# Second half of the first queries: from casting loads on GpSimd's queue to fp32 loads on the sync engine's queue with a cast on VectorE

## The chip, the cores and the metric

The kernel runs on one core of one Trainium2 chip. The metric is the device time of one execution in microseconds. A profile of one execution stands beside the timed runs. Instructions are named by the engine that does them: TensorE (PE, its weight loads PEld), VectorE (DVE), ScalarE (ACT), GpSimd (POOL) and the sync engine (SP), which here only issues DMAs. A DMA issued by GpSimd goes to the queue that the profile calls q0 and may cast on its way; one issued by the sync engine goes to q1.

## The reference

```python
batch, n_heads, seq, head_dim = (4, 8, 768, 64);  n_blocks = 8
P = sort_net
for _ in range(5):                       # rows, then columns, made to sum to one
    P = exp(P - max(P, -1)); P /= sum(P, -1) + 1e-9; P /= sum(P, -2) + 1e-9
k_sorted = einsum('bhij,bhjcd->bhicd', P, k_blocks)      # blocks of 96 tokens
v_sorted = einsum('bhij,bhjcd->bhicd', P, v_blocks)
scores = q_blocks @ k_sorted_blocks.T / sqrt(64)
x = softmax(scores) @ v_sorted_blocks    # within each block
x = x.transpose(0, 2, 1, 3).reshape(3072, 512)
h = x @ w_in                             # 512 x 2048
out = (s * relu(h)**2 + b) @ w_out       # 2048 x 512, float32
```

All inputs are float32.

## The kernel before

The matrices are brought to bf16 and everything large runs on TensorE. The tokens of one batch element are done in two halves of 384 tokens (4 blocks of 96), so that there are eight halves t = 0 to 7. For each half there is an attention part and then two matrix products: `ffn1(t)` (x times w_in, relu, square, into the tile gt) and `ffn2(t)` (gt times w_out, then the store). The order of the instructions on each engine is the order in which the program text calls them: the schedule is written out by hand. Attention pieces of a later half are dropped between the matrix products through dictionaries of `slots`: a slot number says after which step of `ffn1` or `ffn2` a piece is called.

Batch element 0 has nothing before it to hide behind. Its start is: the five normalisations of `sort_net` on 32 partitions (VectorE and ScalarE in turn), the block matrix `PD[0]` on 128 partitions (L270), sorted keys (`k_piece`, tile tp into KS), sorted values (`v_piece`), transposed queries (`q_piece` for blocks 0 to 3, `q_blocks` for blocks 4 to 7 in two calls of two blocks), scores (`s_piece`, `s_banks`), exponentials, and the product with the values (`p_piece`). Then x is transposed (`t_piece`).

Loads of batch 0: the sync engine's queue takes `sort_net` (L79) and v as fp32 (L83). GpSimd's queue takes k (L93) and the first four query blocks (L111), each query block one DMA of 96 partitions by 8 heads by 64 numbers into QTOK, cast to bf16. Then `load_w` issues the weights, also on GpSimd and cast to bf16. `part(a, f)` is one eighth of w_in: rows a and a+1 (of four groups of 128) and a quarter f of the columns. GpSimd does its instructions in order, and `load_w` uses this: the copy L150 reads the block matrix PD[0], so that nothing after it is issued before PD[0] is there, and the copy L154 reads the last column of KS[0], so that nothing after it is issued before the sorted keys are complete. Between these stands the first w_in piece; after the second gate come two more pieces, the four loads of query blocks 4 to 7 (L111), five pieces, and w_out in four DMAs (L165). Loads for batch 1 follow on the same engine (L592 on). Eight semaphores are used in turn for GpSimd's DMAs, so that a DMA waits until the one eight places earlier has landed.

`ffn1(0)` starts with `ahead=3`: for the first three of its eight steps the products with row groups 0 and 1 are done first, then those with groups 2 and 3. Its slot -1 has `t_piece(0, 0, 2)` (transposes of x, evacuated by ScalarE and VectorE), slot ("pre", 1) has `q_blocks(0, 4)`, evacuated by VectorE, and slot 1 has `q_blocks(0, 6)`, evacuated by ScalarE. So on TensorE the 16 transposes of query blocks 4 to 7 (L333) come after the second step and before the third step's row groups 2 and 3. The evacuation and square of each step are

```python
nc.scalar.activation(out=rt, in_=h, func=AF.Relu)                                       # L511
nc.vector.tensor_tensor(out=gt[:, 2 * i:2 * i + 2, :], in0=rt, in1=rt, op=ALU.mult)     # L512
```

and then the slot's pieces are called.

Of the kernel before, what the change touches and what calls it, by code (L numbers as in the profile page):

```python
# [9 lines left out]
FP = mybir.dt.float32  # L10
# [12 lines left out]
def kernel(  # L23
# [12 lines left out]
    nc = tc.nc  # L36

    B, H, S, D = q.shape
    NB = sort_net.shape[-1]
    BLK = S // NB  # L40
# [5 lines left out]
    HB = NB // 2  # L46
    TG = HB * BLK
    C2 = BLK // 2
# [13 lines left out]
    const = ctx.enter_context(tc.tile_pool(name="const", bufs=1))  # L62
# [19 lines left out]
    for c in range(0, C2, CV):  # L82
        nc.sync.dma_start(out=v0f[:, c:c + CV, :].rearrange("p c d -> p (c d)"),  # L83
                          in_=raw[2][0][:, c * D:(c + CV) * D])
# [18 lines left out]
    QTOK = {}  # L103

    def load_q(b, ns=range(NB)):

        if b not in QTOK:
            QTOK[b] = rawp.tile([BLK, NB, H, D], BF, tag="rawq", name="qtok")
        qv = q[b].rearrange("h (n t) d -> t n h d", n=NB)
        for n in ns:  # L110
            nc.gpsimd.dma_start(out=QTOK[b][:, n], in_=qv[:, n])  # L111
# [5 lines left out]
    KS = [const.tile([128, NG, 2, GAP], BF, name=f"ks{i}") for i in range(2)]  # L117
# [17 lines left out]
    load_q(0, range(HB))  # L135
    ones = const.tile([128, 32], BF)
    sel = const.tile([128, 128], BF)
    wi = const.tile([128, NHP, d_ff], BF)
    wo = const.tile([128, NF, d_model], BF)

    def load_w():
        wiv = moe_w_in.rearrange("(a p) f -> p a f", p=128)
        fq = d_ff // 4

        def part(a, f):
            nc.gpsimd.dma_start(out=wi[:, a:a + 2, f * fq:(f + 1) * fq],  # L146
                                in_=wiv[:, a:a + 2, f * fq:(f + 1) * fq])


        nc.gpsimd.tensor_copy(out=ones[:, 0:1], in_=PD[0][:, 0, 0, 0:1])  # L150
        nc.gpsimd.memset(KS[1][:, :, :, C2:GAP], 0.0)
        nc.gpsimd.memset(sel, 0.0)
        part(0, 0)
        nc.gpsimd.tensor_copy(out=ones[:, 0:1], in_=KS[0][:, 0, 0, C2 - 1:C2])  # L154
        part(0, 1)
        part(2, 0)
        load_q(0, range(HB, NB))
        part(2, 1)
        for f in (2, 3):
            for a in (0, 2):  # L160
                part(a, f)
        wov = moe_w_out.rearrange("(f p) n -> p f n", p=128)
        for c in range(4):
            fs = slice(c * (NF // 4), (c + 1) * (NF // 4))
            nc.gpsimd.dma_start(out=wo[:, fs, :], in_=wov[:, fs, :])  # L165
# [14 lines left out]
    def permute(eng, src, cs=slice(0, C2), ds=slice(0, D)):  # L180
# [3 lines left out]
        else:  # L184
# [12 lines left out]
            out=jsel, in_=ident.rearrange("p (h j z) -> p j h z", h=H, j=NB), axis=AX.XY, op=ALU.add),  # L197
        lambda: nc.vector.tensor_reduce(
            out=bm.rearrange("p (e z a) -> p e z a", e=2, z=2),
            in_=idv.rearrange("p a e j z -> p e z a j"), axis=AX.X, op=ALU.add),  # L200
    ] + [
        lambda z=z: nc.vector.tensor_copy(
            out=emat[:, 1:B, z * 64:(z + 1) * 64].rearrange("p b (h j) -> p b h j", h=H),
            in_=ident[0:BH, H:B * H].rearrange("p (b h) -> p b h", b=B - 1).unsqueeze(3).broadcast_to(
                [BH, B - 1, H, NB]))
# [121 lines left out]
    def q_blocks(b, n0, eng):  # L327

        ps = psb.tile([128, 1024], BF, tag="b", name="tqb")
        for n in range(2):  # L330
            for hp in range(NHP):
                c0 = (n * NHP + hp) * BLK
                nc.tensor.transpose(  # L333
                    out=ps[:, c0:c0 + BLK],
                    in_=QTOK[b][:, n0 + n, 2 * hp:2 * hp + 2, :].rearrange("p h d -> p (h d)"),
                    identity=ident[0:BLK, 0:BLK])
        evac(eng, q_tile(b)[:, n0:n0 + 2].rearrange("p n a t -> p (n a t)"),
             ps[:, 0:2 * NHP * BLK])
# [119 lines left out]
    def t_piece(b, half, hp2, eng):  # L458

        x = X[b, half]  # L460
        if hp2 == 0:
            XT[b * 2 + half] = xtp.tile([128, HB, NHP, BLK], BF, tag="xt", name="xt")
        n = HB // len(eng)
        for i, g in enumerate(eng):
            tr = psb.tile([128, 1024], BF, tag="b", name="tr")
            for hp in (hp2, hp2 + 1):
                for m in range(n):
                    c0 = (m * 2 + hp % 2) * BLK
                    nc.tensor.transpose(out=tr[:, c0:c0 + BLK],
                                        in_=x[:, i * n + m, hp * 128:(hp + 1) * 128],  # L470
                                        identity=ident[0:BLK, 0:BLK])
            evac(g, XT[b * 2 + half][:, i * n:(i + 1) * n, hp2:hp2 + 2, :],
                 tr[:, 0:n * 2 * BLK].rearrange("p (n a c) -> p n a c", n=n, a=2))
# [10 lines left out]
    def ffn1(t, slots, ahead=0):  # L484

        gt = gtp.tile([128, NF, TG], BF, tag="gt", name="gt")
        GT[t] = gt
        xt = XT[t]
        H1 = {}

        def part(i, hpl):
            if i not in H1:
                H1[i] = psa.tile([128, 2, 512], FP, tag="a", name="hps")
            for f in range(2):
                for hp in hpl:
                    fc = (2 * i + f) * 128
                    nc.tensor.matmul(out=H1[i][:, f, 0:TG], lhsT=wi[:, hp, fc:fc + 128],  # L497
                                     rhs=xt[:, :, hp, :],
                                     start=(hp == 0), stop=(hp == NHP - 1))

        for i in range(ahead):
            for p in slots.get(i - ahead, ()):
                p()
            part(i, (0, 1))
        for i in range(NF // 2):
            part(i, (2, 3) if i < ahead else range(NHP))
            for p in slots.get(("pre", i), ()):
                p()
            rt = rtp.tile([128, 2, TG], BF, tag="rt", name="rt")
            h = H1.pop(i)[:, :, 0:TG]  # L510
            nc.scalar.activation(out=rt, in_=h, func=AF.Relu)  # L511
            nc.vector.tensor_tensor(out=gt[:, 2 * i:2 * i + 2, :], in0=rt, in1=rt, op=ALU.mult)  # L512
            for p in slots.get(i, ()):
                p()
# [41 lines left out]
    k_piece(0, CK, "D")  # L556
    k_piece(0, 2 * CK, "A")
    load_w()
    v_piece(0, 0, "A")
    q_piece(0, 0, "D")  # L560
# [72 lines left out]
    def SB(b, h, i): return lambda: s_banks(b, h, i)  # L633
    def P(b, h, i): return lambda: p_piece(b, h, i)
    def TP(b, h, i, eng): return lambda: t_piece(b, h, i, eng)
    def TD(b, h): return lambda: t_dma(b, h)
    def PDB(b): return lambda: build_pd(b)
    def QB(b, n0, eng): return lambda: q_blocks(b, n0, eng)


    ffn1(0, {-1: [TP(0, 0, 2, "AD")], ("pre", 1): [QB(0, HB, "D")], 1: [QB(0, HB + 2, "A")],
             2: [SB(0, 1, 0)], 3: [SB(0, 1, 1), P(0, 1, 0)], 4: [SB(0, 1, 2), P(0, 1, 1)],
             5: [SB(0, 1, 3), P(0, 1, 2)], 6: [TP(0, 1, 0, "D"), P(0, 1, 3)]}, ahead=3)
    ffn1(1, {-2: [TP(0, 1, 2, "D")], 1: [masks_z, lambda: take_p(1, B - 1, PB, jselz), PDB(1)], 4: [PDB(2), sum_w],
# [20 lines left out]
    for b in range(B):  # L665
        n = b + 1
# [55 lines left out]
```

## Time and profile before

| what | us |
|---|---|
| median of 3 runs (lowest, highest) | 223.7 (223.66, 227.12) |
| the profiled execution | 224.31 |
| its span, from first to last instruction of the program | 222.5 |
| TensorE busy | 214.8 |
| VectorE busy | 116.6 |
| ScalarE busy | 100.8 |
| GpSimd busy (DMA issues among it) | 55.2 |

The times of the views count from the start of the span; the profiled execution has 1.8 us around it. In a timeline the columns are start, length, engine, line, operation, what is written and read, shape and count, and in brackets the idle time of the engine before it and what ended it. In the DMA views a queue's numbers are packets, megabytes and the share of 16 DMA engines; bytes and packet sizes are those written. Times to landing run from the issue to the last byte's semaphore.

### The profile page before, as it was taken

What the parts mean: (1) busy time and instruction counts of PE and PEld (TensorE: products, weight loads), DVE (VectorE), ACT (ScalarE), POOL (GpSimd) and SP (SyncE); (2) the same over time, 40 slices, a digit from 0 to 9 for tenths busy, and PEclk for the clock granted to TensorE, in tenths of its full rate; (3) what the DMA queues carried; (4) which work ended last, traced back from release to release, by engine and by line L of the source; (5) the groups of instructions that cost most, each with busy time, mean ns of one, the idle gap of its engine ahead of it and who ended that gap; (6) DMA issues with size and microseconds to landing.
All of it is one profiled execution on the core that took longest, in us unless ns stands there. A gap on an engine that the chain in (4) does not pass through costs nothing.

```text
span 222.5 us, 5383 instructions
## 1 busy us (share of the span) xinstructions
PE 214.8 (97%) x2307; PEld 127.1 (57%) x2307; DVE 116.6 (52%) x237; ACT 100.8 (45%) x132; POOL 55.2 (25%) x99
## 2 busy tenths in 40 slices
PE   7898889999999999999999999999999999999993
PEld 8886556655555545655555545665455566654453
DVE  6857547599938556443426746444244734442122
ACT  4688476565442326663354136664325055650000
POOL 8349787359030009100040019000000000000000
PEclk9999999999999999999999999999999999999999
DMA  5999999999979769999669869969423240001212
GB/s 178 258 95 131 163 203 207 219 193 132 177 137 219 147 165 122 156 112 211 160 134 202 209 155 141 151 133 207 114 78 72 102 111 4 0 0 47 94 50 94
DMA packets 66744, 30.51 MB, mean 137 GB/s; under 512 B 57440, under 2 KB 61920, under 8 KB 66528
## 3 DMA queue, kind: packets, MB, share of 16 engines
q0 software_dynamic: 30832, 12.85, 47.3%
q1 hardware_dynamic: 35888, 17.31, 34.4%
q8 instruction: 18, 0.29, 0.5%
q14 instruction: 6, 0.05, 0.1%
HBM read 29.63 MB, written 8.65 MB: 172 GB/s over the span
## 4 chain that ended last, share of the span: by engine, by line
PE 86%; DMA 4%; DVE 4%; POOL 2%; ACT 2%; issue 1%; POOLq 0%
PE ops L522 36%; PE hps L497 36%; DMA wi<-in_moe_w_in_dram 3%; PE pv L441 3%; PE tp L295 2%; PE sc L406 2%; PE ops L536 2%; POOL qtok L111 1%; PE tv L379 1%; ACT ks L284 1%; DMA sne<-in_sort_net_dram 1%; POOL wi L146 1%; PE vob L360 1%; ACT sne L213 1%; DVE rstat L223 1%
## 5 line engine op out<-in xcount | busy, mean ns | idle before, releaser
L497 PE MATMUL hps<-xt,wi 128*128 128x384 bf16 x512 | 86.4, 326 | 1.3 <-DMA wi<-in_moe_w_in_dram 0.9
L522 PE MATMUL ops<-wo,gt 128*128 128x512 bf16 x368 | 84.9, 379 | 0.0
L511 ACT ACTIVATE rt<-hps 128x768 bf16<-128x768 f32 x64 | 51.6, 811 | 52.9 <-PE hps L497 52.0
L497 PEld LDWEIGHTS <-wi 128*128 128x128 bf16 x512 | 48.9, 98 | 35.4 <-issue 2.5
L512 DVE TENSOR_TENSOR gt<-rt 128x768 bf16<-128x768 bf16 x64 | 38.4, 602 | 44.0 <-ACT rt L511 41.9
L522 PEld LDWEIGHTS <-gt 128*128 128x128 bf16 x368 | 34.0, 98 | 37.6
L544 DVE SCALAR_TENSOR_TENSOR ot<-ops,s_bc,bias 128x512 f32<-128x512 f32 (+2 forms) x26 | 18.4, 706 | 33.5 <-PE ops L522 31.5
L411 ACT ACTIVATE at<-sc 96x768 bf16<-96x768 f32 (+1 forms) x28 | 21.2, 806 | 28.4 <-PE sc L406 28.4
L111 POOL DMA_DIRECT2D qtok<-in_q_dram x32 | 24.8, 786 | 7.5 <-DMA wo<-in_moe_w_out_dram 3.7
L449 DVE TENSOR_TENSOR x<-pv,rec 96x512 bf16<-96x512 f32 x32 | 22.0, 687 | 1.1
L441 PEld LDWEIGHTS <-at 112*128 112x128 bf16 (+3 forms) x256 | 10.9, 101 | 4.3 <-ACT vs L284 0.9
L441 PE MATMUL pv<-vs,at 112*128 112x66 bf16 (+3 forms) x256 | 11.7, 195 | 0.8 <-DVE vs L286 0.8
L176 PE MATMUL z<-zeros 128*128 128x142 bf16 (+1 forms) x114 | 11.0, 268 | 1.2 <-DVE zeros L115 1.2
L448 DVE RECIPROCAL rec<-pv 96x8 f32<-96x8 f32 x32 | 6.3, 198 | 11.2 <-PE pv L441 11.2
L284 ACT CAST ks<-tp 128x1024 bf16<-128x1024 f32 x8 | 8.1, 1012 | 7.4 <-PE tp L295 7.4
L176 PEld LDWEIGHTS <-zeros 128*128 128x128 bf16 x114 | 9.5, 116 | 1.4 <-DVE zeros L114 1.0
L661 POOL COPY gate<-gt 128x1 bf16<-128x1 bf16 x2 | 0.4, 191 | 36.8 <-DVE gt L512 36.8
L406 PEld LDWEIGHTS <-ks 64*128 64x128 bf16 x224 | 5.2, 94 | 5.1 <-issue 2.1
L286 DVE CAST ks<-tp 128x1024 bf16<-128x1024 f32 x4 | 4.9, 1222 | 5.7 <-PE tp L295 5.7
L406 PE MATMUL sc<-qt,ks 64*128 64x96 bf16 x224 | 7.5, 204 | 0.2 <-DVE x L449 0.2
L295 PEld LDWEIGHTS <-rawk 128*64 128x64 bf16 x384 | 6.4, 113 | 1.7 <-issue 1.3
L295 PE MATMUL tp<-pd,rawk 128*64 128x64 bf16 x384 | 6.8, 196 | 0.0
(105 smaller groups left out, 117.9 us busy)
## 6 DMA issues: line engine op xcount, KB each, us to landing
out_dram<-ot SPq DMA_DIRECT2D x23, 256.0 KB, 2.1
qtok<-in_q_dram POOLq DMA_DIRECT2D x32, 96.0 KB, 7.2
rawk<-in_k_dram POOLq DMA_DIRECT2D x6, 384.0 KB, 10.3
rawv<-in_v_dram POOLq DMA_DIRECT2D x6, 384.0 KB, 6.6
dv<-VO SPq DMA_DIRECT2D x12, 192.0 KB, 6.4
vs<-dv SPq DMA_DIRECT2D x2, 1152.0 KB, 7.2
wi<-in_moe_w_in_dram POOLq DMA_DIRECT2D x8, 256.0 KB, 8.1
wo<-in_moe_w_out_dram POOLq DMA_DIRECT2D x4, 512.0 KB, 13.8
```

The lines of the kernel that those rows point to most:

```text
L111: nc.gpsimd.dma_start(out=QTOK[b][:, n], in_=qv[:, n])
L176: nc.tensor.matmul(out=Z[0][:, 0:w], lhsT=zeros[:, 0:128], rhs=zeros[:, 0:w], start=True, stop=True)
L295: nc.tensor.matmul(out=ps[e * 64:(e + 1) * 64, c].rearrange("p z g -> p (z g)"), lhsT=src[:, c0 + c, :], rhs=mov[:, e].rearrange("p z g -> ...
L406: nc.tensor.matmul(out=sc[:, e, n * BLK:(n + 1) * BLK], lhsT=KS[b % 2][pr, g0 + n].rearrange("p z c -> p (z c)"), rhs=QT[b][pr, half * HB ...
L411: nc.scalar.activation(out=at, in_=sc[0:rows(b), :, 0:TG], func=AF.Exp, scale=scale)
L441: nc.tensor.matmul(out=pv[0:m, e, n * VW:(n + 1) * VW], lhsT=atf[:, c0:c0 + m], rhs=VS[b > 1][:, e * NG + g0 + n, 0:VW], start=True, stop= ...
L449: nc.vector.tensor_tensor(out=x[:, :, hp * 128:(hp + 1) * 128].rearrange("p n (e d) -> p e n d", e=2), in0=pvv[:, :, :, 0:D], in1=rec.unsq ...
L497: nc.tensor.matmul(out=H1[i][:, f, 0:TG], lhsT=wi[:, hp, fc:fc + 128], rhs=xt[:, :, hp, :], start=(hp == 0), stop=(hp == NHP - 1))
L511: nc.scalar.activation(out=rt, in_=h, func=AF.Relu)
L512: nc.vector.tensor_tensor(out=gt[:, 2 * i:2 * i + 2, :], in0=rt, in1=rt, op=ALU.mult)
L522: nc.tensor.matmul(out=ops, lhsT=gt[:, f, m * 128:(m + 1) * 128], rhs=wo[:, f, :], start=(f == 0), stop=(f == NF - 1))
L544: nc.vector.scalar_tensor_tensor(out=ot[:, ns], in0=ops, scalar=s_bc, in1=BIAS[0][:, ns], op0=ALU.mult, op1=ALU.add)
```

## The change

The copy L154, the second gate on GpSimd, is taken out. The loads of query blocks 4 to 7 leave GpSimd: the sync engine issues four DMAs into a new fp32 tile q0f. A memset of four numbers per partition of q0f stands on GpSimd behind the second w_in piece; since the loads overwrite what it wrote, the first of them waits for it. Two VectorE casts, each of two blocks, bring q0f into QTOK; they stand in slot -1 of `ffn1(0)`, after the transposes of x. Everything else is as it was.

```diff
+    q0f = const.tile([BLK, HB, H, D], FP)
     wi = const.tile([128, NHP, d_ff], BF)
     wo = const.tile([128, NF, d_model], BF)
...
         nc.gpsimd.memset(sel, 0.0)
         part(0, 0)
-        nc.gpsimd.tensor_copy(out=ones[:, 0:1], in_=KS[0][:, 0, 0, C2 - 1:C2])
         part(0, 1)
+        nc.gpsimd.memset(q0f[:, :, 0, 0:1], 0.0)
+        qv = q[0].rearrange("h (n t) d -> t n h d", n=NB)
+        for n in range(HB):
+            nc.sync.dma_start(out=q0f[:, n], in_=qv[:, HB + n])
         part(2, 0)
-        load_q(0, range(HB, NB))
         part(2, 1)
...
+    def cast_q(n):
+
+        nc.vector.tensor_copy(out=QTOK[0][:, HB + n:HB + n + 2], in_=q0f[:, n:n + 2])
+
-    ffn1(0, {-1: [TP(0, 0, 2, "AD")], ("pre", 1): [QB(0, HB, "D")], 1: [QB(0, HB + 2, "A")],
+    ffn1(0, {-1: [TP(0, 0, 2, "AD"), lambda: cast_q(0), lambda: cast_q(2)], ("pre", 1): [QB(0, HB, "D")], 1: [QB(0, HB + 2, "A")],
```

In the changed kernel the lines after these stand three to eight places further down: the transposes L333 are L336, the relu L511 is L514, the square L512 is L515.

## The prediction

> **What bounds the kernel now.** I read the page first: TensorE is busy for 214.8 of 222.5 us, so only time in which TensorE stands still can be won. Next, the chain that ended last in order of time, to see where it leaves TensorE after the start:
>
> ```profile
> 15.88 0.28 issue
> 16.15 1.42 POOL wi L146 x2
> 17.57 3.06 POOL qtok L111 x4
> 20.62 7.77 DMA wi<-in_moe_w_in_dram
> 28.40 0.05 issue
> 28.44 0.82 PE hps L497 x4
> ```
>
> Columns are start, length, what. The changed issues are on the chain: four query loads take GpSimd 3.06 us ahead of the fourth w_in piece, which lands at 28.40 us and releases TensorE. The table of waits prices that:
>
> ```profile
> PE hps L497 <- DMA wi<-in_moe_w_in_dram: 0.9, 1, 0.9
> ```
>
> One wait of 0.9 us is all that an earlier w_in can remove directly. Next, the timelines of TensorE and VectorE at that place:
>
> ```profile
> 24.67 2.17 PE L497 MATMUL hps<-xt,wi 128*128 128x384 bf16 x12
> 26.67 0.85 PE L333 MATMUL tqb<-ident,qtok 96*128 96x96 bf16 x16
> 28.44 0.82 PE L497 MATMUL hps<-xt,wi 128*128 128x384 bf16 x4 [0.93 <-DMA wi<-in_moe_w_in_dram]
> ```
>
> ```profile
> 24.87 0.36 DVE L286 COPY xt<-tr 128x384 bf16<-128x384 bf16 x1 [0.52 <-PE tr L469]
> 27.06 0.56 DVE L512 TENSOR_TENSOR gt<-rt 128x768 bf16<-128x768 bf16 x1 [1.84 <-ACT rt L511]
> ```
>
> TensorE transposes the second queries at 26.67; from 28.44 on it is nearly always busy. So the deadline of the second queries is 26.67 us, in bf16. VectorE has a free slot of 1.84 us just before.
>
> Last, the DMA queues, since a load changes queue. Three stretches: 5 to 9 us (v on the sync engine's queue against k on GpSimd's), 87.5 to 89.5 us (dv stores against query loads), 28.4 to 40 us (weights alone):
>
> ```profile
> q0 software_dynamic: 239, 0.46, 60.5%
> q1 hardware_dynamic: 245, 0.69, 47.9%
> ...
> q0 software_dynamic: 897, 0.11, 85.8%
> q1 hardware_dynamic: 885, 0.17, 76.2%
> ...
> q0 software_dynamic: 2391, 2.36, 123.3%
> ```
>
> q0 is GpSimd's, q1 the sync engine's; the first number counts packets. When both have work, they move the same number of packets, whatever the packets' size. The price of sharing shows in dv, whose transfers need 2.6 us with the engines to themselves and up to 9.7 us beside the query loads:
>
> ```profile
> DMA to landing us min/median/max: 2.6/6.9/9.7
> ```
>
> **What the Trainium skill says.** "DMA: Bandwidth & Descriptors", section "Issuing engines are not separate DMA queues": transfers of all engines run on the same 16 DMA engines and interleave. The trace agrees (dv above). Its section "Queues, rings and completion order": each DMA engine goes round-robin between queues at packet granularity, typically 9 to 17 descriptors a turn. The trace agrees on the turns; its equal counts, with records as large as 3 KB against 2 KB and as small as 192 B against 128 B, look like one record a turn. "VectorE: DVE Perf Modes", section "The perf-mode tier table": an fp32 copy within SBUF runs at 2 elements a cycle; the 512-element cast L619 took 426 ns, which fits. "TensorE: Matmul & The Clock Gate", section "Part 1: The HAM clock gate": after an idle window of some 3.4 us the clock halves until about 3.4 us of activity have passed. The start agrees: 40 of the 142-column matmuls from 1.2 to 5.8 us (115 ns each), 70 from 5.9 to 10.2 us (61 ns each). No pause that long follows in this trace.
>
> **The change part by part.**
>
> *Gate removed.* The copy L154 (0.19 us, 0.94 idle before it, 0.28 after) goes. The first w_in piece is issued from 14.04 to 14.75; the second follows to 15.46 instead of starting at 16.15.
>
> *Four query loads off GpSimd.* 3.06 us of issue go. The eight w_in pieces are issued by about 14.04 + 8 x 0.71 + 0.1 (the new memset, like the 0.09 to 0.20 us memsets of the page) = 19.8 us instead of 25.0. The weights need less of GpSimd and come earlier; this is worth the 0.9 us, no more.
>
> *The four loads on the sync engine's queue.* They wait for the memset at about 15.6 us; nothing else is behind them there until 53.88. With about 1 us from issue to first packet (the 8 KB sort_net load lands after 1.54 us), their packets start at about 16.6 us. Each load has 96 x 8 runs of 64 fp32: 768 packets of 256 B, together 3072, as before, but no longer alone in line: w_in and w_out hold 8 x 256 + 4 x 512 = 4096 packets on GpSimd's queue, some 170 gone by 16.6 us (119 a us, the rate from 15.4 to 20.7 us). If turns are one for one, all 3072 query packets travel beside as many weight packets.
>
> The price of a pair on one engine: a weight packet, 16 engines / (about 2300 data packets in 11.6 us) = 81 ns; a query packet 18 ns (16 engines / 891 packets a us in the dv stretch) to 25 ns[...]. Pair: 99 to 106 ns, I take 103. Each engine has 3072 / 16 = 192 pairs: 19.8 us. Add 1.2 us because weight packets are slower while GpSimd still issues (119 a us against 198), and 0.3 us to the last landing. The fourth query load lands at 16.6 + 19.8 + 1.2 + 0.3 = 37.9 us; the second one, half way, at 28.0.
>
> *The casts.* Two VectorE casts of 96x1024 fp32 to bf16: 426 ns plus 512 more elements at 2 a cycle and 0.96 GHz (267 ns) = 0.69 us each. Had the data been there, they would fit: 25.23 + 1.38 = 26.61, before 27.06. But VectorE takes its work in order, so the second cast stands with its wait in front of gt L512 and of the copies out of PSUM. TensorE meets it sooner: the transposes of the third and fourth block come right after those of the first and second.
>
> *Sum.* First cast 28.0 to 28.7, eight transposes to 29.2; then TensorE idles until the second cast ends, 37.9 + 0.7 = 38.6. Eight transposes (half of 0.85) to 39.05, and the matmuls that started at 28.44 start at about 39.1: +10.7 us. The w_in wait is inside this and gone; all weights they need land before 33 us. TensorE's 9.4 us of idleness lets the clock fall: 3.4 us at half rate lose 1.7 us (bounds 0, if it doesn't fall, and 2.4, half of the 4.7 us at the start). Everything later moves along: TensorE is busy to the end, the later loads come no later than before, and no large wait exists that could give time back. 10.7 + 1.7 = 12.4 us.
>
> The profiled execution took 224.31 us (222.5 span and 1.8 around it): 236.7. The median of the runs is 0.6 below it, so I predict 236.1 us. Bounds of the landing: pairs at 95 ns and no slow phase give 16.6 + 18.2 + 0.3 = 35.1, hence 231.5 without a loss of clock; pairs at 115 ns with 1.2 us give 40.2, hence 239.
>
> **The rivals.**
>
> *The queries come early (the other side).* If a turn of the sync engine's queue takes many small packets, as the skill's 9 to 17 would allow, 3072 packets need little more than their own time, 3072 / 891 = 3.4 us, at most doubled. They land by about 24 us, ahead of 25.23; the casts sit in the free slot, the 0.9 us wait goes. The price turns on one point: landing before about 25.3 us wins, later loses. For it: from 65.5 to 66.3 us the sync engine's queue moved 89 packets of a store while the other moved 22. Against it: the equal counts elsewhere, including loads against loads. Time: 223.7 - 0.9 = 222.8 us, within 2%.
>
> *Uneven sharing.* Two to four query packets a turn: 192 / 3 x (81 + 3 x 20) ns = 9.0 us, plus 1.2 and 0.3: landing at 27.1, resumption at 28.3, about the 28.44 of before; with two a turn, 192 / 2 x 121 ns = 11.6 us, landing 29.7 and resumption 30.9, +2.5: 226.2 us. For it: nothing but the same burst. The clock stays.
>
> *The casts alone.* If they were on the path even with early data, VectorE's row has 1.84 us against 1.38: at most 0.3 us late. Folded into the first rival.
>
> **How the numbers follow.** One for one, 236.1 us (231 to 240): 0.74. Early: 0.13. Uneven, 224 to 231: 0.12. Something else, such as later stages gaining: 0.01. The range 226 to 241 holds the first case and most of the third. 2% is 4.5 us, about what this kernel's measurement tells from no change: slower needs over 228.2 us, the first case and about half of the third, 0.80; same 0.19; faster 0.01, since only 0.9 us is there to win.
>
> **What would show it.** Right: packets of both queues in equal numbers from 17 to 37 us; the fourth query load landing near 38 us; the second cast preceded by a long VectorE idle ended by a DMA; a TensorE gap near 9 us before the L336 transposes; w_in landing by 32 us; the clock row dipping after it. Wrong: query loads landing before 25 us, casts at 25.2 to 26.6, no TensorE gap at 28. If queries land late yet the time doesn't rise, my claim that nothing gives time back is wrong.

## The result and the profile after

The changed kernel is slower: 241.55 us median of six executions (238.28 to 245.31) against 224.62 (223.48 to 227.12) for the kernel before, ratio 1.066 with a 95% interval of 1.055 to 1.077. Ratios here leave out executions that took over 1.5% longer than the fastest of the same kernel (that of the changed kernel rests on 238.28, 239.60 and 240.42), while medians with a lowest and a highest are of all. The two medians differ by a factor of 1.075, and measured once more the ratio was 1.084 (below), so 1.066 is rather low. The prediction was 236.1 us, slower, with a range of 226 to 241 us: the three executions lie in it, the median of all six lies half a microsecond above. The profiled execution took 240.42 us against 224.31 before: 16.1 us more, where 12.4 were forecast.

The page of the changed kernel, four of its rows: busy times, the granted clock, the transposes of the late queries and the casts ahead of them.

```profile
PE 217.0 (91%) x2307; PEld 127.7 (54%) x2307; DVE 116.2 (49%) x239; ACT 101.0 (42%) x132; POOL 52.3 (22%) x95
...
PEclk9999955699999999999999999999999999999999
...
L336 PE MATMUL tqb<-ident,qtok 96*128 96x96 bf16 x16 | 1.6, 278 | 14.3 <-DVE qtok L645 14.3
...
L645 DVE CAST qtok<-q0f 96x1024 bf16<-96x1024 f32 x2 | 2.4, 1208 | 14.2 <-DMA q0f<-in_q_dram 14.2
```

TensorE does the same work in 217.0 us instead of 214.8; most of the 16 us is new idleness: 14.3 us ahead of the transposes, which wait for the casts, which wait for the loads. Three slices of the clock row (digits 5, 5, 6), from about 30 us on, are at about half rate. The chain of waits says the same in order of time:

```profile
15.42 0.13 POOL q0f L156
...
15.56 0.34 SPq L159
...
19.86 21.26 DMA q0f<-in_q_dram
...
41.15 0.70 DVE qtok L645
...
41.90 0.82 PE tqb L336 x8
42.72 1.28 PE hps L500 x4
```

The fourth load lies between 19.86 and 41.12 us. In the timeline of TensorE the one pause of before has become two:

```profile
24.63 2.17 PE L500 MATMUL hps<-xt,wi 128*128 128x384 bf16 x12
33.16 0.82 PE L336 MATMUL tqb<-ident,qtok 96*128 96x96 bf16 x8 [6.36 <-DVE qtok L645]
41.90 0.82 PE L336 MATMUL tqb<-ident,qtok 96*128 96x96 bf16 x8 [7.92 <-DVE qtok L645]
42.52 1.48 PE L500 MATMUL hps<-xt,wi 128*128 128x384 bf16 x4
```

The third step's matmuls, at 28.44 before, start at 42.52, the last transposes still under way (the chain above counts them from 42.72, the end of these): +14.1 us. VectorE's timeline shows the casts:

```profile
31.37 1.73 DVE L645 CAST qtok<-q0f 96x1024 bf16<-96x1024 f32 x1 [6.18 <-DMA q0f<-in_q_dram]
41.15 0.69 DVE L645 CAST qtok<-q0f 96x1024 bf16<-96x1024 f32 x1 [8.05 <-DMA q0f<-in_q_dram]
```

The second takes the 0.69 us of the prediction. The first takes 1.73; it ended at 33.10, 0.55 us after a memset on GpSimd had ended (VO, from 28.61 for 3.94 us, so until 32.55). What the DMA queues moved, from 15.6 to 19.8 us and then from 22 to 36 us (packets, megabytes, share of 16 engines):

```profile
q0 software_dynamic: 433, 0.43, 90.8%
q1 hardware_dynamic: 6, 0.00, 0.3%
...
q0 software_dynamic: 2235, 2.18, 91.6%
q1 hardware_dynamic: 2206, 0.56, 29.7%
```

The second pair is the predicted one: equal numbers of 256 B query packets and 1 KB weight packets (written sizes). The first pair is not: for more than 4 us after the first load was issued at 15.56 us, no more than six query packets moved.

The 16.1 us by place, each as a start after minus the same start before: resumption of the third step 42.52 − 28.44 = 14.1; the second group of scores 46.60 − 30.88 = 15.7, so 1.6 more, most of it because the clock is low; from there to the end 0.7 more in one wait of TensorE, and small differences back.

```profile
PE tqb L336 <- DVE qtok L645: 14.3, 2, 7.9
...
PE hps L500 <- DVE xt L289: 0.7, 1, 0.7
```

The second line is new. VectorE's copy of x stood behind a square L515 that began at 53.40 and took 1.23 us instead of 0.56; four GpSimd copies (L188) ran from 54.08, when an undisturbed square would already have ended.

### The profile page after: what moved, and what is told of

It reads as the page before. It is cut to its first block, busy times and chain, and to the rows that moved or that the text cites. A ratio compares the mean times of both kernels' runs of the same rounds, so it can differ in the third digit from the quotient of the medians.

```text
span 238.7 us, 5387 instructions
## 1 busy us (share of the span) xinstructions
PE 217.0 (91%) x2307; PEld 127.7 (54%) x2307; DVE 116.2 (49%) x239; ACT 101.0 (42%) x132; POOL 52.3 (22%) x95
## 4 chain that ended last, share of the span: by engine, by line
PE 80%; DMA 10%; DVE 4%; SPq 2%; ACT 2%; POOL 1%; issue 1%; POOLq 0%
PE ops L525 34%; PE hps L500 34%; DMA q0f<-in_q_dram 9%; PE pv L444 3%; PE sc L409 2%; PE tp L298 2%; SPq L159 2%; PE ops L539 1%; PE tv L382 1%; DMA sne<-in_sort_net_dram 1%; ACT VP L186 1%; PE vob L363 1%; POOL wi L147 1%; ACT sne L216 1%; PE scb L424 1%
## 5 line engine op out<-in xcount | busy, mean ns | idle before, releaser
L500 PE MATMUL hps<-xt,wi 128*128 128x384 bf16 x512 | 87.9, 330 | 1.0 <-DVE xt L289 0.7
L514 ACT ACTIVATE rt<-hps 128x768 bf16<-128x768 f32 x64 | 51.6, 811 | 54.2 <-PE hps L500 52.8
L500 PEld LDWEIGHTS <-wi 128*128 128x128 bf16 x512 | 49.4, 99 | 35.8 <-issue 3.6
L515 DVE TENSOR_TENSOR gt<-rt 128x768 bf16<-128x768 bf16 x64 | 36.3, 570 | 43.1 <-ACT rt L514 43.0
L111 POOL DMA_DIRECT2D qtok<-in_q_dram x28 | 21.6, 784 | 8.9 <-DVE qt L289 2.7
L336 PE MATMUL tqb<-ident,qtok 96*128 96x96 bf16 x16 | 1.6, 278 | 14.3 <-DVE qtok L645 14.3
L645 DVE CAST qtok<-q0f 96x1024 bf16<-96x1024 f32 x2 | 2.4, 1208 | 14.2 <-DMA q0f<-in_q_dram 14.2
L336 PEld LDWEIGHTS <-qtok 96*128 96x128 bf16 x16 | 1.2, 135 | 14.9 <-DVE qtok L645 14.9
```

## The experiments

Every ratio is against the kernel before, measured beside it. All edits are to the changed kernel, but for the first.

**The gate alone.** To the kernel before:

```diff
-        nc.gpsimd.tensor_copy(out=ones[:, 0:1], in_=KS[0][:, 0, 0, C2 - 1:C2])
```

> The kernel before with one edit: the second gate L154 is gone; the query loads stay on GpSimd's queue. Theory (queries starve behind weight packets on the shared DMA engines): this part of the change is harmless and worth at most the 0.9 us wait for w_in; the fourth w_in piece lands near 27 instead of 28.4 us; 223.0 to 224.3 us where the kernel before takes 223.7 to 224.6. Rival (the early weights do the damage, by crowding the engines): over 228 us.

Ratio 0.9972 (0.9958 to 0.9986), 223.65 us against 224.41. The w_in wait is gone: TensorE went on at 27.70 instead of 28.44. That is the whole worth of the gate, 0.6 us, and this is the fastest version here that computes the right result. The early weights do no damage by themselves.

**The loads ahead of all weights.** The memset and the four loads stand right behind the first gate, ahead of the first w_in piece:

```diff
+        nc.gpsimd.memset(q0f[:, :, 0, 0:1], 0.0)
+        qv = q[0].rearrange("h (n t) d -> t n h d", n=NB)
+        for n in range(HB):
+            nc.sync.dma_start(out=q0f[:, n], in_=qv[:, HB + n])
         nc.gpsimd.memset(KS[1][:, :, :, C2:GAP], 0.0)
         nc.gpsimd.memset(sel, 0.0)
         part(0, 0)
```

> The changed kernel with the memset of q0f and the four loads moved ahead of the first w_in piece (issue near 13.1 us). Theory: until the first weight packet at about 15.3 us the queries have the engines nearly to themselves and move 1000 to 1300 of their 3072 packets; the rest goes one for one at 153 packets a us and lands near 28 us; the third step starts near 29, within 1 us of the kernel before: 224 to 226 us. Rival (the late start of the sync engine's packets is a property of that queue, about 4 us after the issue, whatever else is queued): start near 17.5, landing near 37, about 236 us. Rival (the cast on VectorE costs the time, not the landing): 239 us as changed.

Ratio 1.0068 (1.0041 to 1.0094). Issued from 13.19 us, the loads landed at 16.19, 17.04, 20.70 and 25.38, the last before the expected 28; the casts ran without waiting and TensorE never waited for queries. The queues from 13.2 to 15.2 us:

```profile
q1 hardware_dynamic: 728, 0.18, 40.3%
```

With no weight packets ahead, the first query packets came 1.0 us after the issue, beside the last packets of the first query blocks on GpSimd's queue, and 728 came in 2 us. Here it was the weights that waited: issued at 14.13, their first packets moved at about 16.5, 2.4 us later, where in the changed kernel it was 1.4 us (14.00 to 15.41). So casts and queue are harmless where the loads go first: nearly all of the loss is the lateness of the data. The little that remains is elsewhere. In the profiled execution (229.54 us, where the ratio rests on 225.21 and 225.61) TensorE stands 1.3 us in its first 25 us for a reason that the profile doesn't show, and later waits 2.1 us for one VectorE cast:

```profile
50.27 3.27 DVE L622 CAST cbits<-cfull 128x512 bf16<-128x512 f32 x1
```

It takes 0.43 us in the kernel before. Here it lies beside the four GpSimd copies from 50.12 to 53.25 us, and ends 0.29 us after them.

**The same bytes in an eighth of the packets.** Each partition's 2 KB are read in one piece (the tokens then lie in another order):

```diff
-            nc.sync.dma_start(out=q0f[:, n], in_=qv[:, HB + n])
+            nc.sync.dma_start(out=q0f[:, n].rearrange("p h d -> p (h d)"),
+                              in_=q[0, HB + n].rearrange("(p c) d -> p (c d)", p=BLK))
```

> The changed kernel, but each of the four loads takes the same number of bytes as 96 contiguous runs of 2 KB (other query numbers come into q0f than the reference wants). 384 packets in place of 3072. Theory (a packet has one turn, whatever its size): 24 pairs an engine at about 81 + 90 ns, 4.1 us from the first packet; if the first packet still comes at about 19.5 to 20 us all land by 24.5, the casts fit before 26.7, no gap on TensorE: 223 to 225 us. Rival (the queues share by bytes): as changed, last landing near 41 us, 239 us.

Ratio 0.998 (0.9955 to 1.0005): the loss is gone with the bytes unchanged. The loads landed at 22.53, 24.13, 25.26 and 26.35 us, the last later than the expected 24.5. The start isn't the reason: the packets came at about 19.6 us, 4 us after the issue, as the expectation had allowed for. The first load then took some 3 us to land, the others 1.1 to 1.6 us each. From 22 to 25 us:

```profile
q0 software_dynamic: 325, 0.31, 62.3%
q1 hardware_dynamic: 279, 0.50, 50.7%
```

The queues share by packets, not by bytes: the counts are near each other, while the long packets took 0.50 MB where the weights took 0.31. Sharing by bytes is out.

**Half the packets.** Records of two heads' worth, 512 B, 1536 packets:

```diff
-            nc.sync.dma_start(out=q0f[:, n], in_=qv[:, HB + n])
+            nc.sync.dma_start(
+                out=q0f[:, n].rearrange("p (h c) d -> p h (c d)", c=2),
+                in_=q[0, HB:H, n * 2 * BLK:(n + 1) * 2 * BLK].rearrange("h (p c) d -> p h (c d)", c=2))
```

> The changed kernel with runs of 512 B: the same bytes in 1536 packets (other query numbers come into q0f than the reference wants). Theory (one turn a packet): start near 20 us, 450 packets in the first two us, then 150 a us: last landing near 29.5, the third step's matmuls resume near 30.7, 2.3 us later than before: 226 to 228 us, on the line between 384 packets (224) and 3072 (240). Rival (a threshold between small and large packets, not their number): as one of the two ends, 224 or 240.

Ratio 1.0515 (1.0476 to 1.0554), 235.56 us: a miss in size. The last landing, 31.39 us, was later than the expected 29.5: from 29 us on only some 160 packets of that queue were left, but the last of them took until then. TensorE, with a clock at half rate from 30.3 to 37.2 us, resumed at 33.73. From 22 to 29 us the turns were even once more:

```profile
q0 software_dynamic: 1030, 0.99, 83.7%
q1 hardware_dynamic: 1020, 0.51, 35.3%
```

So the last landing grows with the count of packets at equal bytes: 26.35 us with 384, 31.39 with 1536, 41.12 with 3072. Counted from the first packets near 20 us it still isn't proportional, because the price of a pair grows with the record: from the three counts (16 engines times the stretch, over the query packets) it was about 102 ns with 256 B, 110 with 512 B and 172 with 2 KB. The rest of the miss is VectorE beside GpSimd again: the second cast took 1.64 us beside the memset, and a small product on VectorE at 51.42 us (L254, 128x8) took 3.16 us instead of 0.17 beside the four copies, which cost TensorE a wait of 2.3 us and a second fall of the clock.

**The weights held back.** The other six w_in pieces wait until the queries have landed:

```diff
             nc.sync.dma_start(out=q0f[:, n], in_=qv[:, HB + n])
+        nc.gpsimd.tensor_copy(out=ones[0:BLK, 0:HB], in_=q0f[:, :, 0, 0])
         part(2, 0)
```

> The changed kernel with one more GpSimd copy that reads a column of all of q0f, behind the second w_in piece: the other six w_in pieces are issued only when the queries have landed. Theory: 512 weight packets compete at most; the queries start by 18 us at the latest and land by 21 to 22; the third w_in piece is issued at 22 and lands near 24.5, the fourth near 26, the last near 31.5; the time is that of the kernel before, 223.5 to 226 us. Rival (fp32 loads of 256 B packets on that queue are slow by themselves, near 153 a us): landing past 35, w_in past 38, over 240 us.

Ratio 1.0284 (1.0252 to 1.0317), 229.8 us: a miss, and the most telling one. The queues from 15.6 to 19 us, then from 20 to 25.4 us:

```profile
q0 software_dynamic: 398, 0.39, 93.3%
q1 hardware_dynamic: 1, 0.00, 0.1%
...
q1 hardware_dynamic: 2916, 0.73, 84.7%
...
q0 software_dynamic: 17, 0.01, 1.3%
```

Alone, 2916 query packets went in 5.4 us, 540 a us: small packets on this queue are not slow in themselves. Yet although no weights were issued behind the two pieces, the queries did not start before most of these had gone: by 19.3 us some 435 of their 512 packets had started, and the second piece landed at 21.00. It also answers a guess of the prediction: GpSimd issued nothing from 15.50 to 25.89 us, and the weight packets still went at only 117 a us. The queries landed at 25.32, and the held w_in, issued from 25.89, at 30.12:

```profile
PE hps L501 <- DMA wi<-in_moe_w_in_dram: 4.6, 1, 4.6
```

**One weight piece ahead instead of two.** The block of the experiment above (memset, loads, copy) ahead of the second piece:

```diff
         part(0, 0)
-        part(0, 1)
         nc.gpsimd.memset(q0f[:, :, 0, 0:1], 0.0)
...
+        nc.gpsimd.tensor_copy(out=ones[0:BLK, 0:HB], in_=q0f[:, :, 0, 0])
+        part(0, 1)
         part(2, 0)
```

> A look at when the sync engine's packets start. As the run with the weights held, but the loads are issued behind the first w_in piece alone (issue near 14.9 us) and all other weights wait for them. In the changed kernel the first query packet came about 3.5 to 4 us after the issue at 15.56, in the run with the weights held at about 3.4 us after it, in the run with the loads first within 1 us. If they wait for the weight packets that were queued before them (256 here, done near 17.5 us), they start at 17 to 17.5; if the delay is a fixed 3.4 us whenever the other queue has work, at 18.3; if it were 1 us, at 15.9. The time itself, some 227 to 231 us, says nothing on that.

One execution, 228.75 us. Issued at 15.01, the loads had no packet by 17 us and 303 from 17 to 18:

```profile
q0 software_dynamic: 118, 0.11, 77.2%
q1 hardware_dynamic: 303, 0.08, 35.0%
```

They landed at 19.82 to 22.57. The start comes about 1 us after the issue with no piece ahead, 2.3 us with one (one trace each), 3.4 to 4.3 us with two (several traces). So the delay is not a fixed one of the sync engine's queue; it goes with the weight packets queued when the loads are issued. Here, too, the queries came when most, not all, of the 256 packets had started (some 200), and the piece landed at 18.79.

**The casts where they are used.** Each cast directly ahead of its transposes instead of both in slot -1, run twice:

```diff
-    ffn1(0, {-1: [TP(0, 0, 2, "AD"), lambda: cast_q(0), lambda: cast_q(2)], ("pre", 1): [QB(0, HB, "D")], 1: [QB(0, HB + 2, "A")],
+    ffn1(0, {-1: [TP(0, 0, 2, "AD")], ("pre", 1): [lambda: cast_q(0), QB(0, HB, "D")], 1: [lambda: cast_q(2), QB(0, HB + 2, "A")],
```

> The changed kernel with each cast directly ahead of the transposes that need it, so that VectorE does the squares and evacuations of the first two steps before it waits. Theory (TensorE itself waits for the data, VectorE's order is a side matter): as the changed kernel within 0.5 us in the profile, 239 to 241 us. Rival (VectorE standing in order with everything behind it is what costs): several us less, under 236.

> The kernel with each cast directly ahead of its transposes, once more, for a profile with the clock at full rate up to the wait. Theory (TensorE waits for the data itself): the transposes of the second pair start within 0.3 us of the last query load's landing plus 0.75 us, 240 us. Rival (VectorE's order costs): under 236 us.

243.73 us (241.81 and 245.65) and 242.37 (240.54 and 244.21), two executions each; in neither did the time fall under 236 us. In the second run's profile VectorE did the first step's square at 27.36 us, ahead of both casts, where in the changed kernel it came at 41.76. (The second step's square still stood behind the first cast, at 34.22.) TensorE stood all the same until the data were there:

```profile
41.83 0.82 PE L336 MATMUL tqb<-ident,qtok 96*128 96x96 bf16 x8 [8.12 <-DVE qtok L645]
```

So the place of the casts in VectorE's order is a side matter, to within the spread of these executions.

**The clock kept up.** Zero matrices are transposed in front of the late transposes, 95 and 120 times, so that TensorE is not idle in the wait; run twice:

```diff
+        for _ in range({HB: 95, HB + 2: 120}[n0]):
+            nc.tensor.transpose(out=ps[:, 0:128], in_=zeros[:, 0:128], identity=ident)
```

> The changed kernel with 95 and 120 transposes of a zero tile, 128 columns each, ahead of the two groups of query transposes, to fill TensorE's idle time (some 5.8 and 7.3 us of it at full rate). Theory: the granted clock stays at full rate through the wait, the matmuls after it run at 184 and not 320 ns apart, and 1.5 us come back: profile near 238.9 against 240.4. Rival (the loss of clock is a record, not a cost): no change, 240.4.

> The kernel with TensorE's wait filled by transposes of a zero tile, once more, beside the changed kernel. Theory (the fallen clock costs 1.5 us of matmuls at half rate, as read from the changed kernel's timeline between 42.7 and 46.7 us): 1.5 to 2.5 us faster than the changed kernel, ratio near 1.058, the first matmuls after the wait 184 ns apart. Rival (no cost): same ratio as the changed kernel.

First run: ratio 1.0591 (1.0555 to 1.0626), four executions of 236.39 to 237.82 us, all below the lowest of the changed kernel (238.28); a fifth, the profiled one, took 244.09. Second run: 237.25 to 243.16 us. The times alone don't show the gain: the interval overlaps that of the changed kernel (1.055 to 1.077), and the zero transposes were too many. In the second run's profile they went on until 42.36 us, though the second cast had ended at 40.48, so TensorE resumed 1.9 us later than it could have. The size is read from the matmuls behind them. The clock stays at full rate through the wait, and the late transposes to the second group of scores take 45.41 − 42.36 = 3.05 us:

```profile
42.36 0.51 PE L338 MATMUL tqb<-ident,qtok 96*128 96x96 bf16 x8
...
45.41 0.34 PE L426 MATMUL scb<-qt,ks 64*128 64x96 bf16 x8
```

In the changed kernel the same stretch takes 46.60 − 41.90 = 4.70 us. The lowered clock costs about 1.65 us, by these two profiles.

**The changed kernel once more.** No edit, on another chip, since its spread was wide.

> The changed kernel once more, beside the next run on the same chip. All theories: as measured, ratio 1.055 to 1.077.

Ratio 1.0839 (1.077 to 1.0909), 241.1 to 244.44 us: above the expected 1.055 to 1.077. In its profile the queries landed earlier than before, at 40.02 us, yet TensorE lost more later:

```profile
PE hps L500 <- DVE xt L289: 3.1, 1, 3.1
```

```profile
52.97 3.60 DVE L515 TENSOR_TENSOR gt<-rt 128x768 bf16<-128x768 bf16 x1 [0.56 <-ACT rt L514]
```

The square that took 1.23 us in the first profile takes 3.60 here, until 0.43 us after the four copies, which run from 53.04 to 56.14 us, and the clock falls a second time from 56.8 to 60.2 us.

**Without the four GpSimd copies.** Half of the permuted v columns of batch 1 is left uncopied:

```diff
-    for i in (0, 1, 2, 4):
-        permute(nc.gpsimd, RAW["v", 1], ds=slice(i * 8, (i + 1) * 8))
```

> The changed kernel without the four GpSimd copies L188 that rearrange half of v of batch 1 (32 of its 64 columns are left out, so the values of batch 1 are not those of the reference). In the changed kernel the shifted schedule puts these copies (53 to 58 us) beside the square of ffn1(0)'s seventh step and the evacuation of x behind it on VectorE: that square took 1.23 us in one profile and 3.60 in another instead of 0.56, and TensorE waited 0.7 and 3.1 us for xt, with a second fall of the clock in the latter. Theory (VectorE stands still while GpSimd copies): squares at 0.56 us, no wait for xt, no second fall, 237 to 239.5 us with less spread than the changed kernel's 238.3 to 245.3. Rival (the spread comes from the landing of the queries alone): the wait for xt stays, 240 to 244 us.

Ratio 1.0693 (1.0646 to 1.074), 239.64 to 240.81 us. The squares take 0.56 us, the wait for x is gone, and so is the fall of the clock near 57 us; the spread is 1.2 us where it was 7. The time is slightly above the expected 237 to 239.5, with the last landing at 41.42 us, and two executions of the changed kernel (238.28 and 239.60) were quicker than all four of these, so the landing varies as well. The late queries make the 15 us, and the copies add up to 3 us of waits that differ between executions; how much of the spread they are rests on this one run.

## Why the prediction was right, and where it was short

*Pace of the pairs: right.* The landings at 26.47, 31.25, 36.20 and 41.12 us lie 4.8 to 4.95 us apart; with 48 packets per load on each DMA engine that is 102 ns a pair, predicted 103. "DMA: Bandwidth & Descriptors", section "Queues, rings and completion order", of the Trainium skill has a turn of typically 9 to 17 descriptors; here 2235 packets stand against 2206. The prediction's equal counts are borne out, for 256 B, 512 B and 2 KB records. Its "one record a turn" is not shown: equal turns of several records would give the same counts, so the page isn't contradicted. (The "some 170 gone by 16.6 us" is a slip, 119 a us from 15.4 us make about 140; nothing hangs on it.)

*The 1.2 us for slow weight packets: right in size by luck.* From the first packets at about 19.9 us to the last landing it took 21.3 us, as the prediction's 19.8 + 1.2 + 0.3. But the slow phase lay before the queries' packets, and the run with the weights held shows it without GpSimd issuing. What filled the 1.2 us is the beginning of the sharing, which was not even: from 19.8 to 22 us there were 633 query packets to 242 weight packets. The trace has sixteen completions for each load. Those of the first load lie between 20.98 and 26.47 us, half of them before 22.3; those of the fourth between 36.63 and 41.12. The spread of 5.5 us hardly changes later (4.5), and the last completion, some 1.7 us behind the pace from the first load on, sets the landing. Why the beginning is uneven stays open.

*Start of the packets: the step that failed.* "With about 1 us from issue to first packet" came from a load that was issued into empty queues. Measured: 4.3 us, from 15.56 to about 19.9. This is the whole error of the landing, 41.1 against 37.9, and 3.2 of the 3.7 us by which the profiled execution was longer than forecast; most of the rest is the 0.7 us wait for x. The one microsecond itself was found again where no weights stood ahead (13.19 to 14.19). The experiments with no, one and two weight pieces ahead show that most of what is already queued goes first; even counts come only after that. Why those first weight packets go at only some 100 a us stays open (433 in 4.2 us, where the pair phase has 160 a us of each kind). With the start went the picture of TensorE's wait: one gap near 9 us was forecast, and there were two, of 6.4 and 7.9 us, since the second load, put at 28.0 us, landed at 31.25.

*Clock: right.* The forecast was 1.7 us, of a range of 0 to 2.4. Against the profile with the clock kept up it is 0.3 us from the late transposes to the resumption (41.90 to 42.52, against 42.36 to 42.70) and 1.4 from there to the second group of scores (to 46.60 and 45.41): 1.65 together.

*Casts: right in size, 0.69 us (0.26 more than the 0.43 of the cast with half as many elements); what runs beside them was put at nothing.* GpSimd's memset stretched the first one to 1.73 us, and to 2.96 in the second profile. Here it did not matter, as the second load came 8 us later.

*Gate and weights: right.* No wait for w_in is left; all of it had landed by 33.03 us (32 was forecast), and the gate alone was worth 0.6 us of the 0.9 allowed.

*"Everything later moves along": incomplete.* TensorE is busy to the end and no time came back, but a shift of 16 us brings other pairs of instructions side by side. Before, a square takes 3.41 us beside the same GpSimd copies (52.15 to 55.81 us), and TensorE, by then in the second product, doesn't wait for it:

```profile
51.69 3.41 DVE L512 TENSOR_TENSOR gt<-rt 128x768 bf16<-128x768 bf16 x1 [0.24 <-ACT rt L511]
```

In the changed kernel these copies meet a square of the first product, behind which the copy of the transposed x stands on VectorE: TensorE waited 0.7 us in one profile and 3.1 in the other. "SBUF — State Buffer", section "Who interferes with whom", in the Trainium skill names the rule: a VectorE instruction with two SBUF inputs contends with a GpSimd instruction that reads SBUF, and so does a VectorE copy or cast in a two-port mode with any; who issues first has the ports for its whole instruction. The traces agree that such instructions are held (a square 3.60 us instead of 0.56), in the second profile through all four copies in a row (3.1 us). On who comes first they don't: by the recorded starts the square was ahead of the copies by 0.07 us where it took 3.60, by 0.46 where it took 3.41 (before) and by 0.68 where it took 1.23, and in that first profile a second square ran among the copies in 0.67. What decides is open.

*The rivals.* Queries early: refuted by the counts, and true only with the loads ahead of all weights, where it gave 225.4 and not the 222.8 us of that rival. Uneven sharing: refuted from 22 us on, 2235 to 2206; it held for the first 2 us. Casts alone: with early data they cost no wait, and with late data their place changes nothing that was seen.

## What to carry to other kernels

A small-record load on one queue beside a stream of weights on another was priced here by its number of packets times the price of a pair, not by its bytes: count the records, and make them long or issue them first. Then add what is queued ahead at the moment of issue, since here the sharing began only when most of it had gone (1.0, 2.3 and up to 4.3 us); a latency read where nothing is ahead is too short for that. And after any shift of more than a few microseconds, ask again which VectorE instructions meet which GpSimd ones, since a collision that was hidden can land on the path (0.7 and 3.1 us here).

## What was not expected of the hardware

- A queue that has just got work did not share at once: its first packets came 1.0, 2.3 and up to 4.3 us after the issue, with zero, one and two weight pieces (256 packets each) ahead on the other queue.
- VectorE instructions of 0.17 to 0.69 us lasted 1.2 to 3.6 us when GpSimd ran a memset or copies beside them; most ended within 0.6 us after these.
- Issuing four loads of 768 packets took the sync engine 10.42 us with two weight pieces ahead (15.56 to 25.98), and 2.19 us with none. Behind the same two pieces it took 2.3 us with 384 packets a load (15.67 to 18.00) and 3.7 us with 96 long ones (15.58 to 19.29). So the issue itself can be held up; what decides for how long is not shown.
